# Attention, then routed experts: moving the counts of a threshold search within TensorE's order

## The chip, the cores and the metric

The kernel runs on one core of a Trainium2 chip. The metric is the device time of one launch in microseconds. TensorE (PE in the profile, with its weight loads as PEld), VectorE (DVE), ScalarE (ACT) and GpSimd (POOL) each execute their own list of instructions in the order in which it was written; SyncE (SP) issues DMAs. Semaphores hold an instruction back until what it reads is there, and with it everything behind it on the same engine.

## The reference

```python
# attention: 8 batches, 8 heads, 576 positions, 64 wide; heads 0-3 see a local band of 32, heads 4-7 every 32nd position
x = attention(q, k, v)                     # 4608 tokens x 512
# experts: w_gate 512 x 8, w1 8 x 512 x 1024, w2 8 x 1024 x 512
cap = N // E                               # 576 tokens for each of 8 experts
logits = x @ w_gate
for idx in np.argsort(-logits.flatten()):  # greatest logit first
    tok, e = idx // E, idx % E
    if assigned[tok] >= 0 or counts[e] >= cap:
        continue
    assigned[tok] = e
    counts[e] += 1
for e in range(E):
    mask = assigned == e
    out[mask] = np.maximum(x[mask] @ w1[e], 0.0) @ w2[e]
```

## The kernel before

The first part (to about 175 us) is the attention and the logits, which stay in memory on the chip as `L`, 128 tokens by 36 columns by 8 experts. The second part does the experts, one phase for each of eight, each with all of its 576 tokens.

The greedy loop of the reference is replaced. Of the experts that are still open, the one that fills first is found by a search for the logit at which an expert has 576 tokens that prefer it. That expert is closed, its 576 tokens are taken out, and the next search runs on what is left. So seven searches follow one another; the first (`search0`) runs alone, and the six others (`search`) run beside the matmuls of the phase before. Here search n finds the expert of phase n: search 1 runs beside phase 0, searches 2 to 6 beside phases 1 to 5, and phase 7 gets the expert that is left over. `closed` holds one entry for each expert found, so `len(closed)` is 1 in search 1 and larger in searches 2 to 6.

A search has seven rounds (`rd` 0 to 6; the text below calls them first to seventh). A round has four steps that wait for each other:

- the comparison on VectorE: `cm` holds, for each token and each of 17 thresholds, whether its best logit is above it (line 877 or 880);
- the count on TensorE: nine matmuls with `cm` (line 895);
- the cast `cp` of the counts from PSUM on VectorE (line 899), and the fold on TensorE, four matmuls with the constant `fold` that add up the groups of columns (line 903);
- on VectorE the test against 576 (`g`, line 912) and the greatest threshold reached (`pm`, line 915), with which the next round's `cm` is made.

TensorE's order is written out by a planner in the program itself. `ffn` yields a cost in nanoseconds for each of its matmuls (216 for a second layer's matmul of 512 columns, 123 for a first layer's of 288), and a clock adds them up. Searches and other side chains are generators: each `yield t` means that what follows is written once the clock has moved on by `t`:

```python
                for cost in ffn(ph, *work[ph][:4]):
                    clock += cost
                    for c in list(chains):
                        while c in chains and c[0] <= clock:
                            advance(c)
```

So `T_COUNT`, 3700, is how much matmul work lies between a fold and the next round's count, and `T_SUM`, 1800, between a count and its fold. The costs are fixed numbers, and the planner knows nothing of the other engines. Only TensorE's list is written in this order; VectorE and ScalarE get theirs from a scheduler that puts a search's instructions (`urgent()`) ahead of others where it expects them to be ready. A phase's first layer is `hidden` (line 1260, eight blocks `f` of 24 matmuls, tiles `ph<-xt,w1h` and `ph<-xt,w1l`); of each block ScalarE makes `hh` (line 1267) and VectorE `hl` (line 1268). The second layer is lines 1305 and 1311 (tiles `ph<-w2h,hh` and so on).

Beside the phases the next expert's weights are loaded, scaled and split in two halves each: ScalarE squares them (`jk`), one matmul sums the squares (line 1070, `pr<-ss,ones_b`), VectorE makes the scale (`ss_e`, `w_sw`, lines 212 to 217), and then for each of eight pieces of w1 and of w2 ScalarE makes the upper half (`w1h`, `w2h`) and VectorE the lower (`w1l`, `w2l`, line 1081). The gathered tokens are halved as `xg` (lines 1144 and 1145) and go to `xt` through a transposing DMA. All this VectorE work shares its list with the steps of the search.

Of the kernel before, what the change touches and what calls it, by code (L numbers as in the profile page):

```python
# [49 lines left out]
T_FIRST, T_COUNT, T_SUM, T_PREFIX, T_NEXT, T_HOT, T_DUP = 1100, 3700, 1800, 3900, 2300, 4200, 550  # L50
# [3 lines left out]
MAN, MAN0, MANP = {mybir.EngineType.PE}, {mybir.EngineType.Activation}, (0,)  # L54
T_W20, T_STEP0 = 9000, 1000
X1, X2 = 100, 900
T_TAIL, T_SCAT, T_DUP7 = 1700, 3000, 3000
T_ROWS, T_ROW, T_LOAD, T_ROWS1, T_ROW1, T_LOAD1 = 8000, 2000, 3500, 5000, 1200, 3000
HEAT = (8, 20, 3)
# [79 lines left out]
def band_stride_attention_then_capacity_moe(ctx, tc, qt, kl, ks, nl, ns, wg, w1, w2, cst, out, dbg=None):  # L139
# [647 lines left out]
    scat, closed, first, second, cuts = [], [], [], [], []  # L787
# [8 lines left out]
    def urgent(ph=1):  # L796
        return tc.high_priority(offset=URGENT * (2 if ph == 0 else 1))
# [67 lines left out]
    def pace(t):  # L865
        return t if len(closed) > 1 else t * PACE1

    def search(rm, ohc, more):
        cand, pre, src, top, pm = cand0, pre0, rm, None, None
        ohv = ohc.rearrange("p c e -> p (c e)")  # L870
        for rd in range(R1):
            last = rd == R1 - 1
            t = cand[:, :J1] if last else cand[:, 1:]
            with urgent():
# [7 lines left out]
                cv = cm.rearrange("p c j -> p (c j)")  # L882
                if rd == 0:
                    more()
            yield pace(T_COUNT) + ((X2 if rd == 2 else X1) if len(closed) == 1 else T_FIRST if rd == 0 else 0)
            with urgent():
                if rd and not last:
                    n = 1 if rd == R1 - 2 else J1 + 1
# [8 lines left out]
                cp = rt.tile([128, GC * J1], F16, name="cp")  # L897
                with nc.allow_low_precision(reason="whole numbers up to 384"):
                    nc.vector.tensor_copy(cp, pc)
            yield pace(T_SUM)  # L900
            with urgent():
                for c in range(GC):
                    nc.tensor.matmul(p2, fold[:, c], cp[:, c * J1:(c + 1) * J1], start=(c == 0), stop=(c == GC - 1),
# [309 lines left out]
    def side(src, more):  # L1213
        for ph in range(1, E):
            if ph < E - 1:
                mv, w8 = yield from search(*src[:2], more)
            else:
                mv, w8 = rest()
            while ph >= 2 and ph - 2 not in emitted:
                yield None  # L1220
            if ph == E - 1:
                yield T_LAST
            with urgent():
                ei, code = number(w8)
                oh = mark(code)
            wts = weights(ph, ei)
            slot = yield from slots(ph, *src, code, mv)
            rows_of[ph] = [due_now() + (T_F if 1 < ph < E - 2 else 0), fetch(ph, slot, wts)]
            chains.append(rows_of[ph])
            if ph == E - 2:  # L1230
                yield T_CLOSE6
            if ph < E - 1:
                with urgent():
                    src, todo = close(oh)
                    for f in todo if ph < E - 2 else todo[:3]:
                        f()
                    more = take(slot, src[0])
                yield T_NEXT
# [208 lines left out]
```

## Time and profile before

| | us |
|---|---|
| median of three runs | 649.09 |
| lowest and highest of the three | 644.26 and 656.24 |
| the profiled execution | 645.8 |
| its span, first to last instruction | 644.0 |

The profile shows one execution on the one core. Its times count from the span's first instruction, and 1.8 us of the execution lie outside the span. Searches 2 to 6, which the change touches, lie between 247 and 515 us.

### The profile page before, as it was taken

The numbers are of one execution on the slowest core, as the hardware profiler recorded it, in microseconds if no ns is written. First come the engines' busy times: TensorE is split into PE (matmuls) and PEld (weight loads), VectorE is DVE, ScalarE is ACT, GpSimd is POOL, SyncE is SP. The second block draws the span as 40 slices with busy tenths as digits, with TensorE's granted clock in tenths as the row PEclk, the third lists the DMA queues.
The fourth block names the chain that finished last, engine by engine and source line by source line (L and its number), as shares of the span: only waits on it lengthen the run. The fifth ranks groups of instructions, "written<-read, shape, count | busy, mean of one in ns | idle before, by whom it ended". The sixth has DMA issues, their size and how long they took to land.

```text
span 644.0 us, 19664 instructions
## 1 busy us (share of the span) xinstructions
PE 579.2 (90%) x8221; PEld 368.3 (57%) x8221; DVE 455.8 (71%) x1395; ACT 333.7 (52%) x559; POOL 105.4 (16%) x124
## 2 busy tenths in 40 slices
PE   8789888888747889999999989989989999999996
PEld 4466565666533654476467447547645745755752
DVE  5778788988887987787686776787769557764210
ACT  2685464554303665744852762575286259955211
POOL 2011100111103002300510420050041032032011
PEclk9789999999957999999999999999999999999999
DMA  8788788787406408605821860780394087654001
GB/s 259 195 274 257 235 274 263 241 243 223 128 2 213 148 1 311 156 17 196 226 63 50 285 150 2 266 194 25 103 282 100 1 319 179 246 99 123 1 25 49
DMA packets 78480, 103.40 MB, mean 161 GB/s; under 512 B 41624, under 2 KB 49522, under 8 KB 78391
## 3 DMA queue, kind: packets, MB, share of 16 engines
q1 hardware_dynamic: 70311, 80.59, 42.2%
q0 software_dynamic: 7360, 21.15, 10.4%
q8 instruction: 64, 1.05, 0.7%
q10 hardware_dynamic: 720, 0.39, 0.2%
q14 instruction: 25, 0.20, 0.1%
HBM read 74.58 MB, written 18.87 MB: 145 GB/s over the span
## 4 chain that ended last, share of the span: by engine, by line
PE 35%; issue 19%; DVE 18%; DMA 13%; ACT 6%; POOL 6%; SPq 2%; POOLq 0%; another core or an unknown queue 0%; DVEq 0%; ACTq 0%
PE ph L1260 16%; DMA xr<-x_scr,idx 5%; PE ph L1311 4%; DMA w<-in_w_dram 4%; POOL xr L1155 3%; PE po L426 3%; DVE w1l L1081 2%; PE spa L371 2%; POOL out_dram L1317 2%; DMA v_l<-in_nl_dram 2%; ACT jk L1062 2%; DMA v_s<-in_ns_dram 2%; PE ph L1305 1%; DVE w2l L1081 1%; PE spb L520 1%
## 5 line engine op out<-in xcount | busy, mean ns | idle before, releaser
L1260 PE MATMUL ph<-xt,w1h 128*128 128x288 f16 (+2 forms) x1024 | 173.8, 286 | 2.5 <-DMA xt<-xg 1.5
L1260 PEld LDWEIGHTS <-w1h 128*128 128x128 f16 x1024 | 97.4, 98 | 28.4 <-issue 1.8
L1260 PE MATMUL ph<-xt,w1l 128*128 128x288 f16 (+2 forms) x512 | 109.6, 286 | 0.8 <-DVE w1l L1081 0.8
L1267 ACT ACTIVATE hh<-ph 128x576 f16<-128x576 f32 (+2 forms) x72 | 42.5, 592 | 105.4 <-PE ph L1260 105.1
L1311 PE MATMUL ph<-w2h,hh 128*128 128x512 f16 x256 | 97.1, 379 | 0.0
L1311 PE MATMUL ph<-w2h,hl 128*128 128x512 f16 x256 | 97.1, 379 | 0.0
L1311 PE MATMUL ph<-w2l,hh 128*128 128x512 f16 x256 | 97.0, 379 | 0.0
L1062 ACT ACTIVATE jk<-w 128x1024 f16<-128x1024 f32 x64 | 67.3, 1052 | 50.1 <-DMA w<-in_w_dram 49.1
L1317 POOL DMA_INDIRECT out_dram<-y,idx x40 | 43.9, 1098 | 281.8 <-ACT y L1337 272.3
L1311 PEld LDWEIGHTS <-hh 128*128 128x128 f16 x512 | 48.6, 98 | 56.3 <-issue 4.0
L1268 DVE SCALAR_TENSOR_TENSOR hl<-ph,hh 128x576 f16<-128x576 f32 (+2 forms) x72 | 49.3, 686 | 34.3 <-ACT hh L1267 34.0
L1155 POOL DMA_INDIRECT xr<-x_scr,idx x40 | 42.1, 1052 | 95.4 <-DVE idx L1035 35.3
L1260 PEld LDWEIGHTS <-w1l 128*128 128x128 f16 x512 | 49.3, 98 | 13.2 <-DVE w1l L1081 1.1
L1081 DVE SCALAR_TENSOR_TENSOR w1l<-w,w_sw,w1h 128x512 f16<-128x512 f32 x64 | 46.0, 742 | 3.9 <-ACT w1h L1080 3.0
L1081 DVE SCALAR_TENSOR_TENSOR w2l<-w,w_sw,w2h 128x512 f16<-128x512 f32 x64 | 45.4, 744 | 2.7 <-ACT w2h L1080 2.2
L1080 ACT ACTIVATE w1h<-w,w_sw 128x512 f16<-128x512 f32 x64 | 42.2, 709 | 2.7 <-DVE w_sw L217 1.5
L1080 ACT ACTIVATE w2h<-w,w_sw 128x512 f16<-128x512 f32 x64 | 41.2, 711 | 3.4 <-DVE w_sw L217 2.1
L1337 ACT ACTIVATE y<-ph,so 128x512 f32<-128x512 f32 x32 | 21.7, 679 | 38.8 <-PE ph L1311 20.1
L1311 PEld LDWEIGHTS <-hl 128*128 128x128 f16 x256 | 25.0, 98 | 28.1 <-issue 0.4
L1145 DVE TENSOR_TENSOR xg<-xr,xg 128x512 f16<-128x512 f32 (+1 forms) x37 | 25.4, 688 | 19.4 <-ACT xg L1144 15.0
L476 POOL DMA_DIRECT2D x_scr<-xs x23 | 14.5, 637 | 148.0 <-DVE vsum L311 88.9
L397 ACT ACTIVATE pr<-spa 128x576 f32<-128x576 f32 x32 | 20.7, 646 | 28.0 <-PE spa L394 27.2
(543 smaller groups left out, 876.9 us busy)
## 6 DMA issues: line engine op xcount, KB each, us to landing
w<-in_w_dram SPq DMA_DIRECT2D x64, 512.0 KB
v_s<-in_ns_dram SPq DMA_DIRECT2D x28, 195.0 KB
kl<-in_kl_dram SPq DMA_DIRECT2D x16, 304.0 KB
ks<-in_ks_dram SPq DMA_DIRECT2D x16, 288.0 KB
qs<-in_qt_dram SPq DMA_DIRECT2D x16, 288.0 KB
ql<-in_qt_dram SPq DMA_DIRECT2D x16, 288.0 KB
x_scr<-xl SPq DMA_DIRECT2D x8, 512.0 KB
v_l<-in_nl_dram SPq DMA_DIRECT2D x16, 162.5 KB
```

What stands on the lines that cost most here:

```text
L397: nc.scalar.activation(pr[:, :S].rearrange("k (h n) -> k h n", h=2), u.sp[p][:, :, :HS], AF.Exp, scale=0.125)
L1062: nc.scalar.activation(jk, wf[:, c * n4:(c + 1) * n4].rearrange("p c f -> p (c f)"), AF.Square, scale=1.41422, accum_out=sq[:, c:c + 1])
L1080: a = nc.scalar.activation(hi[:, c, f], wf[:, c, f], AF.Copy, scale=s_)
L1081: b = nc.vector.scalar_tensor_tensor(lo[:, c, f], wf[:, c, f], s_, hi[:, c, f], op0=OP.mult, op1=OP.subtract)
L1145: nc.vector.tensor_tensor(xs[:, 1], xv, xs[:, 0], op=OP.subtract)
L1155: nc.gpsimd.indirect_dma_start(out=xr[:n], out_offset=None, in_=x_rows, in_offset=bass.IndirectOffsetOnAxis(ap=idx[:n, t:t + 1], axis=0))
L1260: nc.tensor.matmul(tile_[:, j, :w], wt[:, d, f * 128:(f + 1) * 128], xt[:, d // 2, xx, d % 2, c], start=(k == 0), stop=(k == 3 * DC - 1))
L1267: nc.scalar.activation(hv, src, AF.Relu)
L1268: nc.vector.scalar_tensor_tensor(lv, src, 0.0, hv, op0=OP.max, op1=OP.subtract)
L1311: nc.tensor.matmul(py, a[:, f, ts_], w[:, f], start=(k == 0), stop=(k == len(todo) - 1))
L1317: st = nc.gpsimd.indirect_dma_start(out=out_rows, out_offset=bass.IndirectOffsetOnAxis(ap=idx[:n, t:t + 1], axis=0), in_=y[:n], in_offset= ...
L1337: nc.scalar.activation(y, py, AF.Copy, scale=so[:, t:t + 1])
```

## The change

Two tables are added, indexed by the round. In searches 2 to 6 the distance from the fold to the third round's count grows by 1500 of the planner's nanoseconds, the distance from there to its fold by 600, and the distance to the counts of the fifth, sixth and seventh rounds falls by 700 each: 2100 more and 2100 less. Searches 0 and 1 stay as they are, and no instruction is added or taken away.

```diff
@@ -54,6 +54,7 @@
 T_W20, T_STEP0 = 9000, 1000
 X1, X2 = 100, 900
+X_COUNT, X_SUM = (T_FIRST, 0, 1500, 0, -700, -700, -700), (0, 0, 600, 0, 0, 0, 0)
 T_TAIL, T_SCAT, T_DUP7 = 1700, 3000, 3000
@@ -882,7 +883,7 @@
-            yield pace(T_COUNT) + ((X2 if rd == 2 else X1) if len(closed) == 1 else T_FIRST if rd == 0 else 0)
+            yield pace(T_COUNT) + ((X2 if rd == 2 else X1) if len(closed) == 1 else X_COUNT[rd])
@@ -897,7 +898,7 @@
-            yield pace(T_SUM)
+            yield pace(T_SUM) + (X_SUM[rd] if len(closed) > 1 else 0)
```

TensorE's order around the matmul that sums the squares of w2 (`pr<-ss,ones_b`), in search 5. Before:

```order
L1311 LDWEIGHTS hh
L1311 MATMUL ph<-w2l,hh 128x512
L1311 LDWEIGHTS hl
L1311 MATMUL ph<-w2h,hl 128x512
L1070 LDWEIGHTS ones_b
L1070 MATMUL pr__7588<-ss,ones_b 128x1
L1260 LDWEIGHTS w1h
L1260 MATMUL ph<-xt,w1h 128x288
```

The same place in the changed kernel:

```order
L904 LDWEIGHTS fold
L904 MATMUL pr__7531<-cp,fold 128x17
L1312 LDWEIGHTS hl
L1312 MATMUL ph<-w2h,hl 128x512
L1071 LDWEIGHTS ones_b
L1071 MATMUL pr__7588<-ss,ones_b 128x1
L1261 LDWEIGHTS w1h
L1261 MATMUL ph<-xt,w1h 128x288
```

The sum of squares stands where it stood, and the third round's fold, which stood ten second-layer matmuls ahead of it, now stands one ahead. In all five searches 25 second-layer matmuls stand between the second round's fold and the third round's count, where 18 stood; 12 between this count and its fold, where 9 stood (in search 6 ten and two of the first layer's); and 25 first-layer matmuls ahead of each of the counts of the fifth, sixth and seventh rounds, where 31 stood.

VectorE's order from the second round's test `g` to the third round's cast `cp`, in search 5. Before:

```order
L912 SCALAR_TENSOR_TENSOR g_7478,ne<-pr__7451,steps 128x17
L1068 TENSOR_REDUCE ss<-sq 128x1
L915 TENSOR_REDUCE pm<-ne 128x1
L1145 TENSOR_TENSOR xg<-xr,xg 64x2x256
L880 SCALAR_TENSOR_TENSOR cm<-pre_7449,pm,rmn 128x612
L890 TENSOR_SCALAR pre_7521<-steps,pm,pre_7449 128x18
L1081 SCALAR_TENSOR_TENSOR w1l<-w_7154,w_sw_7160,w1h 128x4x128 x4
L899 CAST cp<-pr__7523 128x68
```

In the changed kernel:

```order
L913 SCALAR_TENSOR_TENSOR g_7477,ne<-pr__7450,steps 128x17
L1069 TENSOR_REDUCE ss<-sq 128x1
L1146 TENSOR_TENSOR xg<-xr,xg 64x2x256
L916 TENSOR_REDUCE pm<-ne 128x1
L1082 SCALAR_TENSOR_TENSOR w1l<-w_7153,w_sw_7159,w1h 128x4x128
L881 SCALAR_TENSOR_TENSOR cm<-pre_7448,pm,rmn 128x612
L891 TENSOR_SCALAR pre_7529<-steps,pm,pre_7448 128x18
L1082 SCALAR_TENSOR_TENSOR w1l<-w_7153,w_sw_7159,w1h 128x4x128 x3
L900 CAST cp<-pr__7531 128x68
```

One split of w1 (`w1l`) has moved from behind the third round's comparison to ahead of it. In search 4 this stretch is unchanged; in search 3 four splits instead of three stand between comparison and cast.

VectorE's order from `so`, the last step of the scale of w2, to the fifth round's comparison, in search 5. Before:

```order
L1294 TENSOR_SCALAR so<-idx,s_7618 128x5
L1081 SCALAR_TENSOR_TENSOR w2l<-w_7163,w_sw_7169,w2h 128x512 x2
L899 CAST cp<-pr__7635 128x68
L1081 SCALAR_TENSOR_TENSOR w2l<-w_7163,w_sw_7169,w2h 128x512 x2
L912 SCALAR_TENSOR_TENSOR g_7669,ne<-pr__7635,steps 128x17
L1081 SCALAR_TENSOR_TENSOR w2l<-w_7163,w_sw_7169,w2h 128x512
L1268 SCALAR_TENSOR_TENSOR hl<-ph,hh 128x576
L915 TENSOR_REDUCE pm<-ne 128x1
L1081 SCALAR_TENSOR_TENSOR w2l<-w_7163,w_sw_7169,w2h 128x512
L880 SCALAR_TENSOR_TENSOR cm<-pre_7633,pm,rmn 128x612
```

In the changed kernel:

```order
L1295 TENSOR_SCALAR so<-idx,s_7618 128x5
L1082 SCALAR_TENSOR_TENSOR w2l<-w_7162,w_sw_7168,w2h 128x512 x3
L1269 SCALAR_TENSOR_TENSOR hl<-ph,hh 128x576
L900 CAST cp<-pr__7654 128x68
L1082 SCALAR_TENSOR_TENSOR w2l<-w_7162,w_sw_7168,w2h 128x512 x2
L913 SCALAR_TENSOR_TENSOR g_7685,ne<-pr__7654,steps 128x17
L1082 SCALAR_TENSOR_TENSOR w2l<-w_7162,w_sw_7168,w2h 128x512
L916 TENSOR_REDUCE pm<-ne 128x1
L1082 SCALAR_TENSOR_TENSOR w2l<-w_7162,w_sw_7168,w2h 128x512
L881 SCALAR_TENSOR_TENSOR cm<-pre_7652,pm,rmn 128x612
```

Ahead of the fourth round's cast stand three splits and an `hl` where two splits stood, ahead of its `g` five splits and the `hl` where four splits stood; between `g` and the fifth round's comparison the `hl` is gone and two splits stay. In searches 2 and 3 the three splits stand ahead of the cast and two splits and an `hl` between the cast and `g`; in search 6 four splits and an `hl` stand ahead of the cast, three splits between the cast and `g`, and an `hl` and one split between `g` and the comparison.

## Rows read from the trace of the kernel before

**Rows 1.** The page, busy time and share of the span of each engine.

```profile
PE 579.2 (90%) x8221; PEld 368.3 (57%) x8221; DVE 455.8 (71%) x1395; ACT 333.7 (52%) x559; POOL 105.4 (16%) x124
```

**Rows 2.** Windows: length, busy time by engine, TensorE's granted clock, DMA; search 5.

```profile
410.00:464.00 54.00, 52.17 (x448) 32.12 (x446) 40.93 (x126) 29.11 (x51) 11.35 (x10) 1.00 0.48 140
```

**Rows 3.** TensorE's waits from 247 to 515: us in total, times, longest.

```profile
PE pr__6752 L895 <- DVE cm L880: 1.5, 1, 1.5
PE pr__5981 L895 <- DVE cm L880: 1.4, 1, 1.4
PE pr__5137 L903 <- DVE cp L899: 1.3, 1, 1.3
PE pr__8149 L1070 <- DVE p L1026: 1.2, 1, 1.2
PE pr__7523 L895 <- DVE cm L880: 1.1, 1, 1.1
PE pr__8295 L895 <- DVE cm L880: 0.7, 1, 0.7
PE pr__8295 L903 <- DVE cp L899: 0.7, 1, 0.7
PE pr__6752 L903 <- DVE cp L899: 0.7, 1, 0.7
PE pr__7523 L903 <- DVE cp L899: 0.7, 1, 0.7
PE pr__5981 L903 <- DVE cp L899: 0.6, 1, 0.6
...
PE pr__5396 L903 <- DVE cp L899: 0.5, 1, 0.5
```

**Rows 4.** Timeline of TensorE, search 5, third round: start, us, instruction, idle time before.

```profile
426.68 0.38 PE L1311 MATMUL ph<-w2l,hh 128*128 128x512 f16 x1
...
428.62 0.38 PE L1311 MATMUL ph<-w2l,hh 128*128 128x512 f16 x1
430.11 0.25 PE L895 MATMUL pr__7523<-cm,ohn 128*32 128x68 f16 x9 [1.11 <-DVE cm L880]
...
433.09 0.25 PE L903 MATMUL pr__7523<-cp,fold 128*128 128x17 f16 x4 [0.69 <-DVE cp L899]
```

**Rows 5.** Timeline of VectorE, search 5, third to fifth round.

```profile
429.21 0.84 DVE L880 SCALAR_TENSOR_TENSOR cm<-pre,pm,rmn 128x612 f16<-128x612 f32 x1
...
430.17 2.73 DVE L1081 SCALAR_TENSOR_TENSOR w1l<-w,w_sw,w1h 128x512 f16<-128x512 f32 x4
432.82 0.21 DVE L899 CAST cp<-pr__7523 128x68 f16<-128x68 f32 x1
433.38 0.18 DVE L912 SCALAR_TENSOR_TENSOR g<-pr__7523,steps 128x17 f32<-128x17 f32 x1 [0.34 <-PE pr__7523 L903]
...
433.84 0.86 DVE L880 SCALAR_TENSOR_TENSOR cm<-pre,pm,rmn 128x612 f16<-128x612 f32 x1
...
436.03 0.17 DVE L217 TENSOR_SCALAR w_sw<-ss_e 128x2 int32<-128x2 int32 x1
...
436.99 1.41 DVE L1081 SCALAR_TENSOR_TENSOR w2l<-w,w_sw,w2h 128x512 f16<-128x512 f32 x2 [0.27 <-ACT w2h L1080]
...
439.78 0.17 DVE L912 SCALAR_TENSOR_TENSOR g<-pr__7635,steps 128x17 f32<-128x17 f32 x1
...
440.54 0.75 DVE L1268 SCALAR_TENSOR_TENSOR hl<-ph,hh 128x576 f16<-128x576 f32 x1
...
441.95 0.85 DVE L880 SCALAR_TENSOR_TENSOR cm<-pre,pm,rmn 128x612 f16<-128x612 f32 x1
```

**Rows 6.** Timeline of TensorE, search 5, fourth and fifth round.

```profile
435.35 0.17 PE L1070 MATMUL pr__7588<-ss,ones_b 128*128 128x1 bf16 x1
...
437.06 0.27 PE L895 MATMUL pr__7635<-cm,ohn 128*32 128x68 f16 x9
...
439.11 0.25 PE L903 MATMUL pr__7635<-cp,fold 128*128 128x17 f16 x4
...
443.10 0.27 PE L895 MATMUL pr__7712<-cm,ohn 128*32 128x68 f16 x9
```

## The prediction

> **What bounds the kernel now.** I read the page's busy times first, then windows over the phases, then TensorE's waits, and last the timelines of TensorE and VectorE around each wait. The page shows TensorE busy for 90% of the span, VectorE for 71% [rows 1]. In the window of search 5 TensorE has 52.2 of 54 us at a granted clock of 1.00, the upper level (2.4 GHz) [rows 2]. So here TensorE's list runs nearly without a break, and its time is its matmuls and the waits between them. The list of waits from 247 to 515 us is what the change acts on, and the tile's number tells whose wait it is: `pr__5981`, `pr__6752`, `pr__7523` and `pr__8295` are the third rounds of searches 3, 4, 5 and 6. Their counts wait 1.4, 1.5, 1.1 and 0.7 us for the comparison, their folds 0.6, 0.7, 0.7 and 0.7 us for the cast [rows 3]: 4.7 and 2.7, together 7.4 us. The other waits are small: the fold of search 2's second round 1.3 us, of its fifth round 0.5 (`pr__5396`), and a sum of squares in search 6 (`pr__8149`) 1.2 [rows 3]. No count of a fourth to seventh round is in the list. Nearly everything behind these waits hangs on TensorE's place in its list too (the next search, the fetch of the next weights, the gather), so I take a microsecond saved here as a microsecond of the span; the rival that doubts this comes below.
>
> **The third round's count.** Seven more second-layer matmuls stand ahead of it. Their spacing is (428.62 - 426.68) / 9 = 0.216 us [rows 4], so the count comes 1.51 us later in TensorE's list. That covers waits of 1.4, 1.5 and 0.7 in searches 3, 4 and 6 if the comparison stays where it is. In search 5 it doesn't: a split of w1 now stands ahead of it, and four of these take from 430.17 to the cast at 432.82, 0.66 each [rows 5]. Wait there: 1.11 + 0.66 - 1.51 = 0.3. Gain: 4.7 - 0.3 = 4.4 us.
>
> **The third round's fold.** Three more matmuls, 0.65 us, stand between count and fold. What the fold waits for is the cast, which stands behind four splits (430.17, then 432.82) [rows 5]. In search 4 VectorE's order is unchanged, so 0.7 - 0.65 leaves nothing to speak of; in searches 5 and 6 fewer splits stand between, so the wait goes; in search 3 one more split stands ahead of the cast, 0.66 against 0.65 of new cover, and its 0.6 stays. Gain: 2.7 - 0.6 - 0.1 = 2.0 us. The 0.5 us at search 2's fifth round goes as well, since the splits and the `hl` that stood between comparison and cast there now stand before. Gains together: 4.4 + 2.0 + 0.5 = 6.9 us.
>
> **The fourth round and the fifth round's count.** This is the price. The sum of the squares of w2 keeps its place, so the splits of w2 start as before by TensorE's list, but the fourth round now comes later against them, and VectorE takes five or six splits and an `hl` before the fourth round's `g`. Worked out for search 5, from the third round's fold at 0. Before, `g` begins at 433.38 - 433.09 = 0.3 and `cm` at 0.75 [rows 4, 5]; now the three steps of `ss_e` lie among them, so `cm` goes from about 1.1 to 2.0 and `w_sw` follows at 2.2. The first w2 split begins 436.99 - 436.03 = 0.96 after `w_sw` [rows 5], at 3.15; three of them at 0.66 end at 5.15, the `hl` (0.67, by the time to its successor) at 5.8, the cast at 6.0. The fourth round's count stays at 437.06 - 433.09 = 3.97 and its fold 439.11 - 437.06 = 2.05 later, at 6.02 [rows 4, 6]: just met. Two splits more, and `g` begins at 7.3. From `g` to the comparison took 441.95 - 439.78 = 2.17 [rows 5]; without the `hl` between, 1.5; so `cm` runs from 8.8 to 9.65. The fifth round's count followed its fold after 443.10 - 439.11 = 3.99 [rows 6]; six first-layer matmuls fewer, at (437.06 - 435.35) / 14 = 0.122 [rows 6], make 3.26, and it is due at 9.3. So the count waits 0.4 us where it waited for nothing. Search 4 has the same order within a step: 0.4. In searches 2 and 3 the `hl` and one split more stand between cast and `g`: 0.7 each. In search 6 four splits and an `hl` stand ahead of the cast, three more before `g`, and an `hl` behind it: 0.8. Sum: 0.4 + 0.4 + 0.7 + 0.7 + 0.8 = 3.0 us. The bounds: nothing at all, if VectorE keeps ahead, since `g` 0.3 after the fold, 1.5 and 0.85 make 2.65, less than 3.26; and 1.8 a search, 9 in all, if the comparison ends as late after the fold as before (441.95 + 0.85 - 439.11 = 3.69) and a split and an `hl` (1.33) later still. I take 3.0, since the queue that I counted is made of rows of known length.
>
> **Sixth and seventh rounds.** The cover is the same 3.26. No split is left there; `g` 0.3 after the fold, the reduction and the comparison end well before it, also with one `hl` of 0.67 between. Taken at nothing; what hides it is that spare time, and each microsecond by which it is too short would cost up to ten times that, two rounds in five searches.
>
> **The sum.** 645.8 - 6.9 + 3.0 = 641.9 us against the profiled execution. The median of the three runs lies 3.3 us above that execution, the lowest 1.5 below. A median of runs of the changed kernel may lie at the profile or 3.3 above, so I put half of this on it: 643.5 us, less than the 2% (13 us) that a measurement of this kernel can tell from no change.
>
> **Rivals.** *The full gain.* VectorE keeps ahead in the fourth round and only the gains stand: 645.8 - 6.9 = 638.9, on the median's scale 640.5. For it speaks that no count after the third round waits now [rows 3]; against it the count of splits above. Chance 0.17.
>
> *The wait moves and nothing is left.* VectorE does the same work in each phase, 40.9 of 54 us [rows 2], most of it between the second and the fifth round, where it hardly rests [rows 5]. If its list and not TensorE's sets the pace of a search, the microseconds saved at the third round are waited for at the fifth or at the next sum of squares, which already waits 1.2 in search 6 [rows 3]: 645.8, on the median's scale up to 649. Against it: VectorE's idle quarter lies in the same window, and the sixth and seventh rounds let it catch up. Chance 0.18.
>
> The Trainium skill, Perfetto Trace Analysis, section Identifying the Most-Contended Engine, says that matmul busy time is no measure of TensorE, that its weight loads are, and that the engine with the highest occupancy is to be improved first. By that rule, with weight loads at 32.1 of 54 us [rows 2], VectorE would be the contended engine, and shortening TensorE's waits would give the last rival's time. The trace doesn't bear it out here as I read it, since the waits listed are TensorE's, in an otherwise closed row of matmuls.
>
> *Slower.* In the changed order an `hl`, which needs the first block of the first layer and ScalarE's `hh`, stands ahead of the fourth round's cast or `g`. If it comes late, cast, fold, `g` and comparison all queue behind it on VectorE, and TensorE stops at the fifth round's count. From 6.9 / 5 = 1.4 us a search on this eats the gain, that is when the comparison ends more than 4.65 us after the fold (3.69 in search 5 now). At 2.1 us a search: 645.8 - 6.9 + 10.5 = 649.4, on the median's scale up to 652. Against it: the first block is done 25 matmuls, some 3 us, after the sum of squares, and the queue reaches the `hl` only at 5.15. Chance 0.10.
>
> **How the numbers follow.** The forecast, a saving of some 2 to 6 us, has 0.55. The range reaches from the full gain, a little below it, to the slower rival: 637 to 651. All cases lie within 13 us of the time before; what is left for over 2% either way is the spread of the runs themselves (644.3 to 656.2): faster 0.03, same 0.94, slower 0.03.
>
> **What would show it.** In the waits of the changed kernel the counts of the third rounds should be gone but for some 0.3 us in search 5, the folds gone but for search 3, and counts of fifth rounds should stand there with 0.4 to 0.8 each; counts of sixth and seventh rounds should not. Wrong would be: third rounds still waiting (the comparison moved with the count), folds of the fourth rounds waiting long (the `hl`), or the waits gone and the span unchanged (the time is taken back at the weights or at the gather).

## The result, and the profile after

The changed kernel takes 644.07 us, median of 20 runs (635.33 to 653.83), beside 648.59 for the kernel before (20 runs, 643.21 to 656.24). The ratio is 0.9896, 95% interval 0.9866 to 0.9927: some 6.7 us less, clear of no difference and inside 2%. Ratios here and below leave disturbed executions out, here seven of the changed kernel's 20, and of the profiled ones only that of e7_first was disturbed. The medians of all 20 lie 4.5 us apart, a ratio of 0.9930, so the gain is better taken as 4.5 to 6.7 us. The profiled execution took 638.71 us with a span of 636.9, where before it was 645.8 and 644.0. All lines of the program stand one further down: the count is line 896, the fold 904, the cast 900, `cm` 881, `g` 913, the weights' splits 1082, the first layer 1261, the sum of squares 1071.

The page's busy times of the changed kernel, and the window of search 5 (the columns of [rows 1, 2]):

```profile
PE 577.8 (91%) x8218; PEld 367.6 (58%) x8221; DVE 454.8 (71%) x1395; ACT 333.8 (52%) x559; POOL 106.0 (17%) x124
```

```profile
410.00:464.00 54.00, 52.79 (x452) 32.31 (x452) 40.86 (x124) 31.50 (x53) 11.24 (x10) 1.00 0.51 156
```

The work is the same to within 1.4 us on every engine; what shrank is the time between the matmuls. TensorE's waits in the changed kernel, from 247 to 510 us, show which (columns of [rows 3]):

```profile
PE pr__8148 L1071 <- DVE p L1027: 1.7, 1, 1.7
PE ph L1261 <- DMA xt<-xg: 0.9, 1, 0.9
PE pr__5408 L896 <- DVE cm L881: 0.7, 1, 0.7
PE pr__8303 L896 <- DVE cm L881: 0.7, 1, 0.7
...
PE pr__8498 L896 <- DVE cm L881: 0.4, 1, 0.4
PE pr__7531 L896 <- DVE cm L881: 0.4, 1, 0.4
...
PE pr__6951 L896 <- DVE cm L881: 0.3, 1, 0.3
PE pr__6179 L896 <- DVE cm L881: 0.3, 1, 0.3
```

Two things are to be read here against [rows 3]. No fold (line 904) is left in the list, where there were seven: the six that [rows 3] show and the second round's in search 6:

```profile
PE pr__8223 L903 <- DVE cp L899: 0.6, 1, 0.6
```

And of the eight waits that the third rounds had, two counts are left: `pr__7531` (search 5) 0.4 and `pr__8303` (search 6) 0.7. New are the fifth rounds' counts: `pr__5408`, `pr__6179`, `pr__6951` and `pr__8498`, those of searches 2, 3, 4 and 6, with 0.7, 0.3, 0.3 and 0.4. Search 5's fifth round is not there.

Search 5 shows why. Timeline of TensorE in the changed kernel, third to fifth round (columns of [rows 4, 6]):

```profile
424.87 0.25 PE L896 MATMUL pr__7531<-cm,ohn 128*32 128x68 f16 x9 [0.37 <-DVE cm L881]
...
427.66 0.25 PE L904 MATMUL pr__7531<-cp,fold 128*128 128x17 f16 x4
...
431.65 0.27 PE L896 MATMUL pr__7654<-cm,ohn 128*32 128x68 f16 x9
...
433.69 0.25 PE L904 MATMUL pr__7654<-cp,fold 128*128 128x17 f16 x4
...
436.98 0.25 PE L896 MATMUL pr__7722<-cm,ohn 128*32 128x68 f16 x9
```

And VectorE's beside it (compare [rows 5]):

```profile
423.35 0.70 DVE L1082 SCALAR_TENSOR_TENSOR w1l<-w,w_sw,w1h 128x512 f16<-128x512 f32 x1
423.98 0.84 DVE L881 SCALAR_TENSOR_TENSOR cm<-pre,pm,rmn 128x612 f16<-128x612 f32 x1
...
424.94 2.06 DVE L1082 SCALAR_TENSOR_TENSOR w1l<-w,w_sw,w1h 128x512 f16<-128x512 f32 x3
426.93 0.22 DVE L900 CAST cp<-pr__7531 128x68 f16<-128x68 f32 x1
427.94 0.18 DVE L913 SCALAR_TENSOR_TENSOR g<-pr__7531,steps 128x17 f32<-128x17 f32 x1 [0.80 <-PE pr__7531 L904]
...
428.53 0.85 DVE L881 SCALAR_TENSOR_TENSOR cm<-pre,pm,rmn 128x612 f16<-128x612 f32 x1
...
429.50 0.16 DVE L218 TENSOR_SCALAR w_sw<-ss_e 128x2 int32<-128x2 int32 x1
...
430.45 2.08 DVE L1082 SCALAR_TENSOR_TENSOR w2l<-w,w_sw,w2h 128x512 f16<-128x512 f32 x3 [0.25 <-ACT w2h L1081]
432.44 0.75 DVE L1269 SCALAR_TENSOR_TENSOR hl<-ph,hh 128x576 f16<-128x576 f32 x1
433.11 0.22 DVE L900 CAST cp<-pr__7654 128x68 f16<-128x68 f32 x1
...
434.57 0.17 DVE L913 SCALAR_TENSOR_TENSOR g<-pr__7654,steps 128x17 f32<-128x17 f32 x1
...
436.08 0.85 DVE L881 SCALAR_TENSOR_TENSOR cm<-pre,pm,rmn 128x612 f16<-128x612 f32 x1
```

The split that moved ahead of the third comparison (423.35) costs what the prediction put there, and 0.37 us of wait is left. The cast is over at 427.15 and the fold comes at 427.66: half a microsecond to spare where 0.69 were waited. In the fifth round `cm` ends at 436.93 and the count begins at 436.98: met with nothing over.

### The profile page after: what moved, and what is told of

It is laid out like the page before. It is cut to its first block, busy times and chain, and to the rows that moved or that the text cites. A ratio compares the mean times of both kernels' runs of the same rounds, so it can differ in the third digit from the quotient of the medians.

```text
span 636.9 us, 19662 instructions
## 1 busy us (share of the span) xinstructions
PE 577.8 (91%) x8218; PEld 367.6 (58%) x8221; DVE 454.8 (71%) x1395; ACT 333.8 (52%) x559; POOL 106.0 (17%) x124
## 4 chain that ended last, share of the span: by engine, by line
PE 44%; DVE 21%; issue 19%; DMA 7%; ACT 5%; POOL 4%; SPq 1%; POOLq 0%; DVEq 0%; ACTq 0%
PE ph L1261 14%; PE ph L1312 9%; PE spa L372 4%; PE po L427 3%; DVE w2l L1082 3%; DMA xr<-x_scr,idx 3%; POOL xr L1156 2%; PE ph L1306 2%; POOL out_dram L1318 2%; DVE cm L881 2%; DMA xt<-xg 1%; PE spb L521 1%; PE spa L395 1%; DMA v_l<-in_nl_dram 1%; DMA w<-in_w_dram 1%
```

## The experiments

The theory at the start, by its two parts: the third round waits because its count and fold stand too near behind the steps that VectorE must do for them, so distance there is what gains, and distance is free to give in the last three rounds but for a new queue at the fifth. Its rivals: that only the place of the rounds in the phase counts (beside which of VectorE's other work they fall), and that any lengthening or shortening of a search is paid for at its end. Each expectation names its theories by letters and says what they are. The first four kernels, from the changed one, line 57 (the label of each stands behind its line):

```diff
-X_COUNT, X_SUM = (T_FIRST, 0, 1500, 0, -700, -700, -700), (0, 0, 600, 0, 0, 0, 0)
+X_COUNT, X_SUM = (T_FIRST, 0, 1500, 0, 0, 0, 0), (0, 0, 600, 0, 0, 0, 0)           # e1_late
+X_COUNT, X_SUM = (T_FIRST, 0, 0, 0, -700, -700, -700), (0, 0, 0, 0, 0, 0, 0)       # e2_close
+X_COUNT, X_SUM = (T_FIRST, 0, 1500, 0, -700, -700, -700), (0, 0, 0, 0, 0, 0, 0)    # e3_nofold
+X_COUNT, X_SUM = (T_FIRST, 0, 1500, 0, 0, -1400, -700), (0, 0, 600, 0, 0, 0, 0)    # e4_sixth
```

**Only the third round further (e1_late).**

> The third round's count and fold further behind (1500 and 600), the counts of the last three rounds left where they were. Theory A (each wait of TensorE in searches 2 to 6 is time, and the three closer counts pay for the two later steps by keeping the search's end in its place): the fifth rounds' waits, 1.7 us in the changed kernel, are gone, but each search now ends about 2.2 us of matmuls later, the next one starts later for that, and the last fold of search 6 stands 11.8 us later in TensorE's list than in the changed kernel. Phase 6, which waits 1.3 us for its tokens there, waits some 8 to 13 us: 645 to 650 on the scale where the changed kernel's profiled execution is 638.7, about as slow as before or slower. Rival B (only the third round matters, the closer counts are a loss that bought nothing): 1.7 us faster than the changed kernel, 637.

690.55 us (689.52 to 697.96, 5 runs), ratio 1.0665 (1.0577 to 1.0754). The sign was right and the size wrong by 40 us or more (645 to 650 was forecast). Neither third nor fifth rounds wait any more, but every search is 2.1 of the planner's microseconds longer, the next one starts where it ends, and by search 6 the last fold stands 11.8 us of matmuls later in TensorE's list. What hangs on a search's end (the experts' weights and rows, which are loaded by what it finds) is then not there. TensorE's waits of this kernel, 247 to 530 us:

```profile
PE ph L1261 <- DMA xt<-xg: 16.4, 6, 5.8
PE pr__7563 L1071 <- DVE ss L1069: 6.4, 1, 6.4
PE pr__8307 L1071 <- DVE ss L1069: 4.5, 1, 4.5
```

The third round's distance is therefore no gain by itself; it has to be paid back within the same search.

**Only the last three closer (e2_close).**

> Only the counts of the last three rounds closer, the third round as before. Theory A: the third rounds' waits are back, 4.7 us at the counts and 2.7 at the folds; fifth rounds wait 0 to 0.8 each, some 1.6 in all; the searches end up to 10 us of matmuls earlier than in the changed kernel, so phase 6's wait of 1.3 goes: about as before, 645 to 647. Rival C (what made the change faster is that the last three rounds are closer and the chain of searches shorter): most of the gain is here already, 640 or less.

659.39 us (655.91 to 670.21, 5 runs), ratio 1.0149 (1.0059 to 1.024): slower, where about no change was expected; rival C, which put most of the gain here, is out. The third rounds' counts wait nearly as before (4.1 us), their folds less (0.7), and now the searches run ahead: 10 us of matmuls earlier by search 6, with 6.15 us of waits at second rounds' folds and 3.0 at the matmuls that make the list of rows. A search that is too short costs as well, if less.

**Without the 600 at the fold (e3_nofold).**

> As the changed kernel, but without the 600 ns more between the third round's count and its fold. Theory A: the third rounds' folds wait for the cast again, 0.6 to 0.7 us in three or four of the five searches, 2 to 2.7 us in all; the search is 0.65 shorter, so the last one ends 3.5 us earlier in TensorE's list and phase 6's 1.3 us goes: 639.5 to 641. Rival D (the cast was late only because the count was late, so the 600 is idle): no wait at these folds, 637.5.

656.42 us (650.4 to 660.27, 5 runs), ratio 1.0104 (0.9996 to 1.0212). This missed: 639.5 to 641 was forecast, and the profiled execution took 653.86. The folds of the third rounds wait 2.35 us, as forecast; their counts wait 4.9 us as well, which no theory had. The search is 0.6 us shorter, 3.5 us of matmuls by search 6, and there the second round's `g` came 6.3 us after its fold, behind a halving (`xg`) whose other half ScalarE made late, as it waited 3.3 us for the gather. The worst of it in TensorE's waits of this kernel:

```profile
PE pr__8285 L896 <- DVE cm L881: 3.9, 1, 3.9
PE pr__6755 L904 <- DVE cp L900: 1.8, 1, 1.8
```

Distance alone does not say this; the place beside the gather may.

**The fifth round's share taken from the sixth (e4_sixth).**

> As the changed kernel, but the fifth round's count is where it was before and the sixth round's count is 1400 closer, not 700; the search keeps its length. Theory A: the fifth rounds' waits (0.7, 0.3, 0.3, 0.0, 0.4 us, 1.7 in all) are gone; the sixth round's comparison ends 1.6 to 2.3 us after its fold and has 2.5 us of cover, so nothing waits there: 637. Rival E (VectorE is behind and the wait only moves): the same 1.7 us or more stand at the sixth rounds' counts, 638.7 to 640.

645.87 us (639.62 to 651.64, 11 runs), ratio 0.9931 (0.9884 to 0.9977). The fifth rounds' waits are gone, and the sixth rounds, now 1400 closer, have none in their place, as the queue of VectorE has none of the weights' splits left there. So rival E is out. The time is not to be told from the changed kernel's, since the two intervals overlap: the 1.3 to 1.7 us are less than these runs can tell. The profiled execution took 643.35 us, where 637 was forecast, as other waits came in (second rounds' folds 3.0, third rounds 1.8, sums of squares 2.3).

Four more asked whether the distance or the place does it, and whether half does half:

```diff
+X_COUNT, X_SUM = (T_FIRST, 0, 1500, 0, -700, -700, -700), (0, 0, 600, 0, 0, 0, 0)        # e5_again: the changed kernel
+X_COUNT, X_SUM = (T_FIRST, 0, 750, 0, -350, -350, -350), (0, 0, 300, 0, 0, 0, 0)         # e6_half
+X_COUNT, X_SUM = (T_FIRST - 2100, 0, 1500, 0, 0, 0, 0), (0, 0, 600, 0, 0, 0, 0)          # e7_first
+X_COUNT, X_SUM = (T_FIRST + 2100, 0, 0, 0, -700, -700, -700), (0, 0, 0, 0, 0, 0, 0)      # e8_place
```

e7_first keeps the distances and brings the third fold back to its old place in the phase; e8_place keeps the place of that fold and takes the distances away.

> The changed kernel once more, unchanged, beside the others of this group. It tells how far a profiled execution of one program repeats: the waits of TensorE in searches 2 to 6 (8.9 us over all from 247 us on in the first profile) and the stretch from search 2's first count to the span's end (385.9 us; before 391.9). Theory A, whose sums go by waits of single profiles, needs the third rounds' counts and folds free of waits again, and the stretch within 2 us.

> Half of the change: 750 and 300 more for the third round, 350 less for each of the last three counts. Theory A: the third round has 0.65 us more cover for its count and 0.2 for its fold, so the counts wait some 0.8, 0.9, 0.5 and 0.1, the folds 0.4 each; the fifth rounds wait 0.3 less than in the changed kernel. Between the two: 388 to 390 for the stretch from search 2's first count to the end. Rival G (the gain comes from an accident of VectorE's order, not from the cover): no place between the two, as fast as one or the other or slower than both.

> The third round as in the changed kernel (1500 and 600 further from what stands ahead of it), but the 2100 are taken from the first round, not from the last three, so the search keeps its length, and in TensorE's list the third round's count stands 0.65 us ahead of its place in the kernel before. Theory A (what counts is the cover between fold and count): third rounds free of waits as in the changed kernel, fifth rounds free too (cover 3.9 us), 384.5 for the stretch. Theory F (the third round's comparison is pinned by the token rows: the second round's test stands behind their halving on VectorE, which waits for the gather, so what counts is the count's place in the list, not its distance from the fold): the counts wait 0.6 us more than before, 1.3 to 2.1 each, 6.5 to 7.5 in all: 391 to 394.

> The distances around the third round as before, but the first round's count stands 2100 later and those of the last three rounds 700 closer, so the third round's count stands 2.15 us later in TensorE's list than before and the search keeps its length. Theory A: the counts and folds of the third rounds wait as before, 4.7 and 2.7, the fifth as in the changed kernel: 393. Theory F (place in the list): the second round's test now comes later by itself, when the token rows are there, so the third round has no wait or little, as in the changed kernel: 386 to 388; the second round's folds may wait less as well.

The kernel before had a median of 656.29 us beside these (25 runs on another chip). e5_again: 657.08, four runs from 646.64 to 660.78, too few for a ratio; they show no gain. e6_half 657.69, ratio 1.0033 (0.9988 to 1.0077). e7_first 657.55, ratio 0.9941 (0.988 to 1.0003, from four of its ten executions; the median of all ten lies 1.3 us above the kernel before). e8_place 657.27, ratio 1.0042 (0.9989 to 1.0096). None of the four is faster by these runs, the changed kernel itself included.

The stretch from search 2's first count to the end took 392.5, 399.7, 403.5 and 399.8 us in this order, and every forecast of it missed: 385.9 within 2 us for e5_again, 388 to 390 for e6_half, 384.5 or 391 to 394 for e7_first, 393 or 386 to 388 for e8_place. Half of the change came out slower than the kernel before (391.9) and the changed one (386.0 and 392.5), which is what rival G allowed and theory A did not. What is left to read are the waits by round. TensorE's waits at the third round and at the second, from its timelines in searches 2 to 6, one execution of each kernel, in us:

| | distance | place | third count | third fold | second count | second fold |
|---|---|---|---|---|---|---|
| before | old | old | 4.65 | 2.68 | 0 | 1.90 |
| e11_before_again | old | old | 4.20 | 1.99 | 0 | 3.58 |
| e7_first | new | old | 0 | 8.76 | 0 | 3.42 |
| e8_place | old | new | 2.44 | 0 | 3.57 | 6.31 |
| changed | new | new | 1.09 | 0 | 0 | 0 |
| e5_again | new | new | 0 | 0.55 | 0 | 3.38 |
| e6_half | half | half | 4.24 | 0.79 | 0 | 6.07 |

So neither theory holds alone. With the distance but not the place, the counts' waits go and the folds wait 2.3 to 2.8 us each in three searches; with the place but not the distance, the folds' waits go, the counts keep half of theirs, and the second rounds wait 9.9 us, where theory F expected less. Of these only the kernel with both has its third rounds nearly clear, 1.1 and 0.6 us in its two executions. That is what single executions show; the times of these four don't confirm it. Nor did any kernel hold VectorE's list as it was: each new order of TensorE gave another order of the splits and halvings too, as in the changed kernel itself, and what this alone does is not shown. What e7_first's fold waited for in search 5 shows on VectorE; its count had run at 439.81, and its fold at 445.54 had waited 2.77:

```profile
439.62 0.69 DVE L1146 TENSOR_TENSOR xg<-xr,xg 128x512 f16<-128x512 f32 x1 [1.35 <-issue]
441.27 0.75 DVE L1082 SCALAR_TENSOR_TENSOR w1l<-w,w_sw,w1h 128x512 f16<-128x512 f32 x1 [0.96 <-ACT w1h L1081]
442.60 0.68 DVE L1146 TENSOR_TENSOR xg<-xr,xg 64x512 f16<-64x512 f32 x1 [0.57 <-ACT xg L1145]
...
443.94 1.41 DVE L1082 SCALAR_TENSOR_TENSOR w1l<-w,w_sw,w1h 128x512 f16<-128x512 f32 x2
445.26 0.22 DVE L900 CAST cp<-pr__7514 128x68 f16<-128x68 f32 x1
```

Halvings and splits stand ahead of the cast. The idle time ahead of two of them is that of an input from ScalarE; ahead of the first the profile names nothing. Two kernels were to take the halvings off VectorE, from before and from the changed one:

```diff
-            nc.vector.tensor_tensor(xs[:, 1], xv, xs[:, 0], op=OP.subtract)
+            nc.gpsimd.tensor_tensor(xs[:, 1], xv, xs[:, 0], op=OP.subtract)
```

> The kernel before, with the lower half of the gathered rows (the subtraction that makes xg) on GpSimd instead of VectorE, for all phases from 1 on; TensorE's order is the same. Theory F (the third round's comparison and cast are late because the second round's steps stand behind these halvings, which wait for the gather): with the halvings out of VectorE's list the waits at second and third rounds, 4.65 + 2.68 + 1.90 us in the kernel before, fall below 2.5 in all. Theory H (VectorE's splits of the weights alone make the queue): the counts and folds of the third round go on waiting, 5 us or more. The total may be worse in either case: GpSimd has the gathers and the stores in the same list and may be slower at this step, which delays the transposes and a phase's start (1.5 us at phase 6 before).

> The changed kernel with the same move of the halvings to GpSimd. Theory F: nothing is left for the change to cover, so third rounds don't wait and the fifth rounds' price stays, 1 to 1.7 us: this kernel is the same as the kernel before with the same move, or 1 to 2 us slower than it. Theory H: it is 4 to 6 us faster than that one.

668.63 us (ratio 1.0231, 1.0162 to 1.0299) and 663.27 (1.0154, 1.01 to 1.0208), both slower than the kernel before, so the trial disturbs what it measures. By its number theory F fails: second and third rounds of e9_pool_before wait 17.5 us, where less than 2.5 was forecast. The change is still worth 5.4 us between the two (four runs each), as theory H has it, though VectorE's list has no halving in it. But it isn't shown that a queue of the weights' splits does this. The third rounds keep 8.5 of their 10.6 us of waits in e10_pool_after; the folds of the second rounds go from 7.0 to 3.5, and the time at the lower clock (the table of stretches below) from 13.7 to 6.8. And GpSimd put a new delay in, as VectorE and GpSimd of e9_pool_before show side by side:

```profile
448.92 3.70 DVE L890 TENSOR_SCALAR pre<-steps,pm,pre 128x18 f32<-128x18 f32 x1
449.19 3.38 POOL L1145 TENSOR_TENSOR xg<-xr,xg 128x512 f16<-128x512 f32 x3
```

An instruction of 0.29 us took 3.70 while GpSimd halved three tiles. **The kernel before once more** was run beside them, to see which waits repeat:

> The kernel before once more, unchanged, with a profile of its own beside the others. If waits of single profiles repeat, its counts and folds of third rounds wait 4.7 and 2.7 us again, within 1.5 us in all, and its fourth to seventh counts don't wait; the stretch from search 2's first count to the end is 390 to 394 if no half-clock stretch falls into it.

650.89 us (647.49 to 659.65, 10 runs), ratio 0.9999 (0.9947 to 1.0051). TensorE's waits of this execution at the third rounds, and the longest:

```profile
PE pr__6676 L903 <- DVE cp L899: 2.2, 1, 2.2
PE pr__7523 L895 <- DVE cm L880: 1.5, 1, 1.5
...
PE pr__5981 L895 <- DVE cm L880: 1.4, 1, 1.4
PE pr__8295 L895 <- DVE cm L880: 1.3, 1, 1.3
...
PE pr__7523 L903 <- DVE cp L899: 0.7, 1, 0.7
PE pr__8295 L903 <- DVE cp L899: 0.7, 1, 0.7
PE pr__5981 L903 <- DVE cp L899: 0.6, 1, 0.6
```

The third rounds wait 6.2 us where they waited 7.3, to a tenth the same in search 3 and at the folds of searches 5 and 6; search 4 is missing, since its second round's fold (`pr__6676`) waited 2.2 first. No fifth round's count is there. The third rounds' waits thus belong to the order; those of the second rounds' folds come and go with the execution, in either kernel.

**No halving on VectorE, and none on GpSimd.** The last kernel, from the one before, lets ScalarE write zeros in their place, so the first layer's result lacks the lower halves of the tokens:

```diff
-            nc.vector.tensor_tensor(xs[:, 1], xv, xs[:, 0], op=OP.subtract)
+            nc.scalar.activation(xs[:, 1], xv, AF.Copy, scale=0.0)
```

> The kernel before, with VectorE's subtraction of the gathered tokens (line 1145, five a phase, 0.69 us each of 128x512) taken off its list: ScalarE writes zeros into the lower half of xg instead, so the lower halves of the tokens are left out of the first layer's result; TensorE's order and work are unchanged. It asks whose queue holds up the second and third rounds. Theory H1 (the splits of the weights make VectorE's queue, and the third round simply stands too near behind its fold in TensorE's list): the third rounds' counts and folds still wait 5 us or more in all in searches 3 to 6, as the 7.3 and 6.2 us of the two profiles of this kernel; the time as before within 0.5%. Theory H2 (the halvings that wait for the gather and for ScalarE make it): with them gone the waits of second and third rounds together, 9.2 and 9.8 us there, fall below 2.5 us, and the time below the kernel before by some 5 to 7 us (0.992 to 0.989 of it), as the changed kernel. Theory D (ScalarE, which gets 5 more copies a phase, becomes late with w2h and hh): new waits at the first layers or the second, and a time above the kernel before.

655.91 us, ratio 0.9999 (0.995 to 1.0048). The third rounds of searches 3 to 6 wait 5.65 us (count 1.40, fold 4.25), second and third together 7.8: by its numbers the first theory. VectorE's list shows that the third came in as well; the third round in search 6:

```profile
486.15 0.75 DVE L1081 SCALAR_TENSOR_TENSOR w1l<-w,w_sw,w1h 128x512 f16<-128x512 f32 x1 [2.44 <-ACT w1h L1080]
...
488.38 0.75 DVE L1081 SCALAR_TENSOR_TENSOR w1l<-w,w_sw,w1h 128x512 f16<-128x512 f32 x1 [1.03 <-ACT w1h L1080]
489.05 0.22 DVE L899 CAST cp<-pr__8295 128x68 f16<-128x68 f32 x1
```

The cast now stands behind splits that wait for ScalarE, 12.6 us of such idle time in the five searches where the kernel before had 0.5; theory D had put ScalarE's lateness at the layers. So taking one tenant off VectorE's list does not free the round: the next one, held by another engine, takes the place. Which of them costs how much in the kernel before isn't settled by this.

## Why the prediction held, step by step

The time came at 644.07 for 643.5, from a median before that read 648.59 for 649.09: 4.5 us saved for 5.6. That it is so near is in part luck. The sum gave 641.9 for the profiled execution, which took 638.71, and half of the distance between profile and median was added by choice. What speaks for the mechanism is the terms. In the stretch from search 2's first count to the end (391.9 us before, 386.0 after) the steps stand as follows; the second pair is e11_before_again and e5_again:

| step | forecast | profiled pair | second pair |
|---|---|---|---|
| third rounds' counts, gain | 4.4 | 4.65 - 1.09 = 3.56 | 4.20 - 0 = 4.20 |
| third rounds' folds, gain | 2.0 | 2.68 - 0 = 2.68 | 1.99 - 0.55 = 1.44 |
| search 2's fifth fold, gain | 0.5 | 0.52 | 0.52 |
| fifth rounds' counts, price | 3.0 | 1.67 | 1.27 |
| sum | 3.9 | 5.09 | 4.89 |

**The gains** were 6.9 by the forecast and 6.8 and 6.2 by the traces. Their parts: search 5's count kept 0.37 for a forecast 0.3, in one execution; search 6's count kept its 0.7 in one execution, which was to be covered; search 3's fold, which was to keep its 0.6, kept none in one execution and 0.5 in the other. The cover of 1.51 us for search 6's count held only if the comparison stayed where it was. It did not: it ended 4.80 us after the second round's fold before, 6.33 in the changed kernel and 4.69 in e5_again. In the changed kernel the second round's `g` stood on VectorE behind this halving, which waited for ScalarE's half:

```profile
475.59 0.69 DVE L1146 TENSOR_TENSOR xg<-xr,xg 128x512 f16<-128x512 f32 x1 [1.23 <-ACT xg L1145]
```

**The price** is the term that was mis-sized, by nearly half. It was worked out from search 5, and there the queue was the one foreseen, link by link, with one link wrong. From the third fold at 427.66, `g` begins at 0.28 (forecast 0.3), the fourth count at 3.99 (3.97), its fold at 6.03 (6.02), the fifth count at 9.32 (9.3). But `w_sw` comes at 1.84 where 2.2 was put, mostly since the three steps of `ss_e` put the comparison off by 0.12 us (it begins at 0.87, before at 0.75) and not by 0.35; the three splits begin at 2.79 (3.15), the second `g` at 6.91 (7.3), and `cm` ends at 9.27 (9.65). The whole queue is 0.4 early, which is just the 0.4 that search 5's count was to wait. Search 3 waited 0.26 (0.7), search 4 0.28 (0.4), search 6 0.39 (0.8), search 2 0.74 (0.7).

These have other reasons. In searches 3 and 4 `ss_e` came behind the comparison, `w_sw` at 2.16, and the fifth comparison ended 9.60 us after the third fold in both, nearly the 9.65 that was put for search 5, with the count due at 9.4 and not 9.3. The prediction put 0.3 more on searches 2 and 3 for an `hl` and a split more between cast and `g`; but that `hl` had only moved there from ahead of the cast, and five splits and an `hl` stand ahead of `g` in all four of searches 2 to 5. In search 3, third fold at 322.12:

```profile
324.28 0.17 DVE L218 TENSOR_SCALAR w_sw<-ss_e 128x2 int32<-128x2 int32 x1
...
330.87 0.85 DVE L881 SCALAR_TENSOR_TENSOR cm<-pre,pm,rmn 128x612 f16<-128x612 f32 x1
```

In search 6 the steps of `ss_e` were over before the third fold and the splits began at 1.85, which made up for most of the two that stand there in addition. Search 2's 0.7 was met by luck: its third `g` began 0.75 us after the fold and not 0.3, behind a split of w1; with 0.52 in e5_again it waited 0.50.

**Sixth and seventh rounds** wait for nothing, as put; e4_sixth shows that the sixth had 0.7 more to give.

**A microsecond of wait is one of span.** From the third profile on this can be tested. With the TensorE waits over 0.15 us from search 2's first count on, and half of the time that TensorE then spent at the lower clock (1.2 of 2.4 GHz) up to its last matmul, taken off that stretch, this is left, in us:

| | stretch | waits | lower clock | left |
|---|---|---|---|---|
| before | 391.9 | 12.7 | 0 | 379.2 |
| changed | 386.0 | 7.7 | 0 | 378.3 |
| e11_before_again | 394.3 | 13.5 | 3.4 | 379.1 |
| e5_again | 392.5 | 10.3 | 6.8 | 378.8 |
| e4_sixth | 388.9 | 10.5 | 0 | 378.4 |
| e3_nofold | 398.7 | 15.8 | 6.8 | 379.5 |
| e2_close | 403.6 | 20.4 | 6.8 | 379.8 |
| e12_nohalving | 396.8 | 15.7 | 3.4 | 379.4 |
| e9_pool_before | 406.4 | 21.8 | 13.7 | 377.7 |
| e10_pool_after | 400.4 | 18.4 | 6.8 | 378.6 |

e6_half (380.9), e7_first (383.8) and e8_place (375.5) lie further off, the last two because their search 2 begins elsewhere in TensorE's list: from one and the same matmul on, they come to 379.6 and 378.1, the ten of the table to 377.6 to 379.6, and e6_half to 380.7. e1_late, much of whose waiting falls into the lower clock, can't be reckoned so. The table shows that the time is TensorE's matmuls, waits and clock; whether a wait that is saved comes back elsewhere shows in the sum of the waits alone. In the profiled pair that rival finds no support: of the 5.1 us saved, 4.9 are missing from the sum of all waits, and 5.9 from the stretch. In the second pair it isn't out: of 4.9 saved, 3.2 are missing from the waits and 1.9 from the stretch, and the four runs of e5_again show no gain. The rival of the full gain lies about as near in the price as the forecast, 1.67 and 1.27 between nothing and 3.0. The slower one had no part: no fourth round's fold waited.

**What the sum had no term for.** Second rounds' folds (1.90 to 0 here, 3.58 to 3.38 in the second pair; the prediction had seen search 2's 1.3 and not search 6's 0.6), sums of squares and first layers (2.74 to 4.34), and 1.2 us ahead of search 2, where both kernels are alike. Together they made the profiled pair look like 7.1 us. They belong to the execution and not to the change as far as the second pair shows; that the second pair's stretches differ by 1.9 us only comes from 1.9 us more of other waits in e5_again (2.0 at a sum of squares, 1.0 ahead of a second layer's matmul) and from its 6.8 us at the lower clock, beside 3.4. Why a second round's fold waits in some executions stays open: the cast that it needs stood on VectorE for something that the view doesn't name, as this row of VectorE's timeline in e5_again shows:

```profile
434.24 0.23 DVE L900 CAST cp<-pr__7450 128x68 f16<-128x68 f32 x1 [3.91 <-remote]
```

The semaphores in that trace narrow it down. The cast waits for one of TensorE's semaphores, and begins 0.02 us after an update of it at 434.22, which stands 5.1 us after the end that the profile gives the count. As far as these records go, VectorE's queue did not hold this cast; why the update came so late no run here shows.

It stays open too whether the gain is 1% on each chip: the four runs of e5_again don't show it.

## What to carry to other kernels

In a list that one engine works off in order, putting a late step further back is not a gain by itself: the same distance has to be taken from steps of the same loop that have it to spare, so that the loop's end stays where it was. Either side of that transaction alone cost 1.5 to 6.7% here; both together gained about 1%, 0.7% with the distance taken from other steps (e4_sixth), and nothing that four runs on another chip could show. Which step has some to spare is read from the other engine's queue at that step, link by link, in durations of the trace, and one link that is 0.4 us off decides a wait of 0.4 us. Distance and place are two settings: look at what else falls due on the waited-for engine at the new place, most of all work that itself waits for a transfer.

## What the runs showed of the hardware

**A wait can cost twice.** In e5_again TensorE stood from 431.1 to 434.5 us at the fold of a second round, and after it the granted clock fell to the lower level. Windows of that execution (columns of [rows 2]):

```profile
431.10:434.50 3.40, 0.04 (x1) 0.00 (x0) 0.26 (x2) 2.31 (x4) 1.61 (x2) 1.00 1.24 228
434.50:437.90 3.40, 3.38 (x14) 1.32 (x14) 3.40 (x10) 3.08 (x5) 0.00 (x0) 0.65 0.72 187
437.90:441.30 3.40, 3.40 (x15) 1.45 (x14) 2.89 (x5) 0.69 (x1) 0.81 (x1) 0.85 0.55 102
441.30:444.70 3.40, 3.40 (x28) 1.51 (x27) 0.23 (x1) 0.00 (x0) 0.35 (x1) 1.00 0.22 82
```

After the wait the clock is 0.65 and 0.85 in two windows of 3.4 us, so (0.35 + 0.15) x 3.4 = 1.7 us of matmul time are lost on top of the 3.4 waited, and then it is 1.00 again. In e1_late a wait of 10.45 us ahead of a sum of squares, up to 592.44, was followed by a window (592.4 to 600) with a clock of 0.70. Not every wait is followed so: waits of 2.0 and 2.2 us in e4_sixth, at a second round's fold and a sum of squares, were not.

**The start of search 2 moves by itself.** TensorE's list ahead of it is the same in the changed kernel, e5_again and e1_late, and yet its first count came between 251 and 265 us, with a granted clock over the first 240 us of 0.93 in the changed kernel (start 251.0), 0.89 in e5_again (261.3) and 0.86 in e1_late (264.6). That spread is larger than the effect measured here; whether it makes up most of the spread of the runs wasn't tried.

**GpSimd's halving** of a tile takes 1.16 us (median of 37; three of 128x512 in a row 3.38) where VectorE takes 0.69, and beside it a VectorE instruction that else takes 0.29 us took 3.70.
